# adaLN block on one Trainium2 core: the last tile's two stores move from SyncE to ScalarE, and the register that selects the general path is loaded three tiles sooner

## Chip, cores and metric

The kernel runs on one core of a Trainium2 chip. The metric is the device time of a launch in microseconds (us): the median of the runs of a kernel. The profile is one more execution, recorded instruction by instruction; its span reaches from the first recorded instruction to the last.

## What is computed

A transformer block over 2048 rows of 512 values, in bfloat16: an attention half with a softmax feature map and linear attention, and a gated feed-forward half. Both read a layer norm whose scale and shift come from the conditioning vector `c`. Cut to what matters:

```python
mod = (silu(c) @ w_mod).reshape(1, 6, 1, -1)          # sa, ca, ga, sb, cb, gb
h = layernorm(x) * (1 + ca) + sa
x = x + ga * A(h)            # q, k, v; phi = softmax(+-(q or k) @ w_phi); linear attention; @ wo
h = layernorm(x) * (1 + cb) + sb
x = x + gb * B(h)            # (sigmoid(h @ w_gate) * (h @ w_up)) @ w_down
```

The softmaxes are taken without subtracting the maximum when a bound on the logits is small enough. The kernel computes that bound on the chip (`bound_tasks`, line 896) and leaves a 0 or 1 in the one-element tile `flag` (line 915). With 0 the result stands; with 1 a general path, appended to the program behind a conditional (line 1279), recomputes everything. In the runs here the flag is 0, so the general path is jumped over.

## The kernel before

The 2048 rows are 16 tiles of 128 rows. The attention half walks over these tiles; then `downstream` runs the feed-forward half over six chunks of 1, 1, 2, 4, 4 and 4 tiles. For each chunk, TensorE makes the gate and up products for 11 slices of the 1376 hidden columns (line 850), ScalarE takes a tanh of the gate (line 854), VectorE multiplies (line 859). Then TensorE accumulates the down product of each tile over the 11 slices into a PSUM bank `y` (line 873), VectorE adds the residual and writes the bfloat16 tile `ot` (line 882, task `fin`), and SyncE stores `ot` to the output in HBM (line 884, task `st`). The last tile, t = 15, is done in two column halves of 256 (`cuts`), so it has two adds and two stores of 64 KB; all other tiles have one of each, 128 KB a store. There are two `ot` buffers.

The order of the work is planned on the host. Each step is a task with the engines that may run it and their estimated times, the keys that it reads and writes, the buffers that it holds and a due time; `Graph.order` simulates the engines and gives one list, and `emit` calls the tasks' functions in that order. An engine executes its own instructions in the order in which they were emitted; the Tile layer adds the semaphore waits. "SP" in the plan is SyncE, "ACT" ScalarE.

`load_flag` is no task of its own. It is called from inside the function of a `fin` task (line 881 stands in it) and emits a `TENSOR_LOAD` of `flag` into a register on every one of the five engines, at whatever place each engine's stream has reached (line 891). The register is read only by the compare-and-branch at line 1279. After that, each engine waits for its own work to finish and jumps over the general path to the block at the end of the program (reported as line 1306), where the engines meet. SyncE alone waits before its jump for all eight semaphores on which DMAs report, whichever engine issued them.

Of the kernel before, what the change touches and what calls it, by code (L numbers as in the profile page):

```python
# [12 lines left out]
ACT = mybir.ActivationFunctionType  # L13
# [5 lines left out]
NT = S // P  # L19
# [407 lines left out]
def kernel(  # L427
# [5 lines left out]
    pe, act, dve, pool, sp = nc.tensor, nc.scalar, nc.vector, nc.gpsimd, nc.sync  # L433
# [54 lines left out]
    o_v = out.flatten_outer_dims().rearrange("(n p) d -> p n d", p=P)  # L488
# [24 lines left out]
    def h2v(b):  # L513
        return h2_slots[b.slot].rearrange("p s k n -> p (s k) n")[:, 0:KT]

    def engine(e):
        return {"PE": pe, "ACT": act, "DVE": dve, "POOL": pool, "SP": sp}[e]
# [7 lines left out]
    def bank(name, shape=None, dtype=FP32):  # L525
        return Buf("bank", shape or [P, 512], dtype, name)
# [77 lines left out]
    def downstream(G, eT, base, first):  # L604
# [18 lines left out]
        for p, tiles in enumerate(UNITS):  # L623
# [81 lines left out]
            for q, t in enumerate(tiles):  # L705
                ub = []
                if merged:
                    us = [Buf("r2k", [P, H, DH], FP32, "u") for _ in range(2)]
                    for i in range(3):
                        for s in (i,) if i < 2 else (0, 1):  # L710
                            nh, h0, c0 = (24, 0, 0) if i < 2 else (8, 24, s)
# [127 lines left out]
        for k in range(NC):  # L839
            n = CHUNKS[k] * P  # L840
            h2k = [("h2", p, j) for p in range(len(UNITS)) if chunk_of[UNITS[p][0]] == k for j in range(KT)]
            for ft in range(FT):
                fsz = P if ft < FT - 1 else F_LAST
                g_ps, u_ps = bank("g_ps"), bank("u_ps")
                dd = gdue[k, ft]

                def f_g(e, w, ps, ft=ft, fsz=fsz, k=k, n=n):
                    h = h2v(h2[k])
                    for j in range(KT):
                        pe.matmul(ps[:fsz, 0:n], lhsT=w[:, j, ft * P:ft * P + fsz], rhs=h[:, j, 0:n], start=(j == 0), stop=(j == KT - 1))  # L850
                dur = 0.216 * n / 128
                tg = Buf("tg", [P, 512], BF16, "tg")
                G.add(f"g{k}.{ft}", {"PE": dur}, lambda e, f=f_g, ps=g_ps: f(e, wg_sb, ps), r=h2k + ["wg"], w=[("g", k, ft)], bufs=[h2[k], g_ps], due=dd)
                G.add(f"tg{k}.{ft}", {"ACT": 0.13 + n * 0.00083}, lambda e, tg=tg, g_ps=g_ps, fsz=fsz, n=n: act.activation(tg[:fsz, 0:n], g_ps[:fsz, 0:n], ACT.Tanh, scale=0.5),  # L854
                      r=[("g", k, ft)] + (["tsw"] if first else []), w=[("tg", k, ft)], bufs=[g_ps, tg], due=dd + 0.5)
                G.add(f"u{k}.{ft}", {"PE": dur}, lambda e, f=f_g, ps=u_ps: f(e, wu_sb, ps), r=h2k + ["wu"], w=[("up", k, ft)], bufs=[h2[k], u_ps], due=dd + 0.01)

                def f_hm(e, k=k, ft=ft, fsz=fsz, n=n, tg=tg, u_ps=u_ps):
                    dve.scalar_tensor_tensor(hm_all[:fsz, hm[k].slot, ft, 0:n], tg[:fsz, 0:n], 1.0, u_ps[:fsz, 0:n], op0=ALU.add, op1=ALU.mult)  # L859
                G.add(f"hm{k}.{ft}", {"DVE": 0.1 + n * 0.00115}, f_hm, r=[("tg", k, ft), ("up", k, ft)] + (["wmod_free"] if first else []),  # L860
                      w=[("hm", k, ft)], bufs=[tg, u_ps, hm[k]], due=dd + 1.0)
            nd = CHUNKS[k] * FT
            for tl in range(CHUNKS[k]):
                t = C0[k] + tl
                cuts = [(0, 256), (256, 512)] if t == NT - 1 else [(0, 512)]
                ot = Buf("ot", [P, D], BF16, "ot")
                for c0, c1 in cuts:
                    y = bank("y_ps")
                    for ft in range(FT):
                        fsz = P if ft < FT - 1 else F_LAST  # L870

                        def f_y(e, k=k, tl=tl, ft=ft, fsz=fsz, y=y, c0=c0, c1=c1):
                            pe.matmul(y[:, 0:c1 - c0], lhsT=hm_all[:fsz, hm[k].slot, ft, tl * P:(tl + 1) * P], rhs=wd_sb[:fsz, ft, c0:c1], start=(ft == 0), stop=(ft == FT - 1))  # L873
                        i = tl * FT + ft
                        due = gdue[k + 1, i * FT // nd] + 0.02 if k + 1 < NC else ydue + i * 0.216
                        G.add(f"y{t}.{ft}" + ("b" if c0 else ""), {"PE": 0.216 * (c1 - c0) / 512 + 0.0012}, f_y, r=[("hm", k, ft), ("wd", ft)],
                              w=[("y", t, c0)] + ([("ycap", t % 2)] if ft == 0 and c0 == 0 else []), bufs=[hm[k], y], due=due + c0 * 0.01)

                    def f_fin(e, t=t, y=y, ot=ot, c0=c0, c1=c1):
                        if first and t == NT - 1 and c0 == 0:  # L880
                            load_flag()
                        dve.tensor_tensor(ot[:, c0:c1], y[:, 0:c1 - c0], x1[t][:, c0:c1], op=ALU.add)  # L882
                    G.add(f"fin{t}" + ("b" if c0 else ""), {"DVE": 0.08 + 0.61 * (c1 - c0) / 512}, f_fin, r=[("y", t, c0), ("ycap", t % 2)], w=[("ot", t, c0)], bufs=[y, x1[t], ot], due=due + 1.0 + c0 * 0.01)
                    G.add(f"st{t}" + ("b" if c0 else ""), {"SP": 0.35}, lambda e, t=t, ot=ot, c0=c0, c1=c1: sp.dma_start(o_v[:, t, c0:c1], ot[:, c0:c1]),
                          r=[("ot", t, c0)], w=[("out", t, c0)], bufs=[ot], due=due + 2.0 + c0 * 0.01, nbytes=128e3 * (c1 - c0) / 512)


# [2 lines left out]
    def load_flag():  # L890
        fv_box.append(nc.values_load(flag[0:1, 0:1], min_val=0, max_val=1,
                                     skip_runtime_bounds_check_because="written as 0 or 1"))
# [26 lines left out]
    G = Graph(CAPS, DUE, REL, ENG)  # L919
# [271 lines left out]
    for cq in range(4):  # L1191
        for blk in range(4):
# [12 lines left out]
            G.add(f"qe{cq}{blk}", {"ACT": 1.0}, f_qe, r=[("q", cq, blk)], w=[("eT", cq, blk)], bufs=[qp, eT[cq]], due=due)  # L1205

    downstream(G, eT, GB, True)
    bound_tasks(G, GB + 95.0)
    order = G.order()
# [55 lines left out]
    for cq in range(4):  # L1265
        for tl in range(4):
            t = 4 * cq + tl
# [3 lines left out]
            def f_t(e, ph=ph, tp=tp):  # L1271
                for g in range(NG):
                    pe.transpose(tp[:, g, :], ph[:, g * P:(g + 1) * P], ident[:])
            G2.add(f"gT{t}", {"PE": 0.5}, f_t, r=[("gphq", t)], w=[("gT", t), "chain"], bufs=[ph, tp], due=100.0 + t)
            G2.add(f"gTc{t}", {"ACT": 1.0}, lambda e, cq=cq, tl=tl, tp=tp: act.copy(eT2[cq][:, :, tl * P:(tl + 1) * P], tp[:]),
                   r=[("gT", t)], w=[("eT", cq, tl)], bufs=[tp, eT2[cq]], due=100.0 + t)
    downstream(G2, eT2, 200.0, False)
    order2 = G2.order()
    with tc.If(fv_box[0] > 0, preferred_fallthrough_block=False):
# [31 lines left out]
```

## Time and profile before

| | us |
|---|---|
| median of 5 runs | 219.29 (218.65 to 220.47) |
| the profiled execution, its own device time | 219.26 |
| span of the profiled execution | 217.5 |
| TensorE busy in the span | 202.8 (93%) |
| VectorE busy | 165.5 (76%) |
| ScalarE busy | 112.9 (52%) |
| GpSimd busy | 98.1 (45%) |
| last matmul ends, about | 211.0 |
| last add on VectorE | 211.05 to 211.47 |

How to read it: the profiled execution is 1.7 us longer in device time than its span, and within 0.03 us of the median of the runs. Instructions are named by engine, line and operation. A "q" behind an engine's name (SPq, DVEq, PEldq) marks records of its sequencer: DMA issues, register loads, semaphore waits and branches, which are not counted as busy. The time "to landing" of a DMA runs from the start of its issue to the completion that its semaphore shows. Besides instructions, the trace holds one record for each DMA packet with its queue, size, start and duration; queue 1 carries the DMAs that SyncE issues, queue 10 those that ScalarE issues, queues 8 and 14 bring instructions.

### The profile page before, as it was taken

The numbers are of one execution on the slowest core, as the hardware profiler recorded it, in microseconds if no ns is written. First come the engines' busy times: TensorE is split into PE (matmuls) and PEld (weight loads), VectorE is DVE, ScalarE is ACT, GpSimd is POOL, SyncE is SP. The second block draws the span as 40 slices with busy tenths as digits, with TensorE's granted clock in tenths as the row PEclk, the third lists the DMA queues.
The fourth block names the chain that finished last, engine by engine and source line by source line (L and its number), as shares of the span: only waits on it lengthen the run. The fifth ranks groups of instructions, "written<-read, shape, count | busy, mean of one in ns | idle before, by whom it ended". The sixth has DMA issues, their size and how long they took to land.

```text
span 217.5 us, 4285 instructions
## 1 busy us (share of the span) xinstructions
PE 202.8 (93%) x1495; PEld 113.2 (52%) x1519; DVE 165.5 (76%) x441; ACT 112.9 (52%) x285; POOL 98.1 (45%) x125
## 2 busy tenths in 40 slices
PE   7983999999999999999999999999999999999970
PEld 2731455565565568867965444554444444444540
DVE  3898689998769999888798898999897961344230
ACT  3889499998978984424563223463112721243000
POOL 4547989999999963743542221324024100000000
PEclk9999699999999999999999999999999999999996
DMA  6999993794000111250321301133111231000111
GB/s 180 368 255 231 347 172 32 242 376 183 0 3 0 29 24 29 41 107 0 75 48 50 74 3 24 31 89 91 28 33 24 48 85 40 0 0 0 51 51 35
DMA packets 32511, 19.02 MB, mean 87 GB/s; under 512 B 21761, under 2 KB 30434, under 8 KB 32482
## 3 DMA queue, kind: packets, MB, share of 16 engines
q1 hardware_dynamic: 31952, 18.65, 32.9%
q8 instruction: 14, 0.23, 0.5%
q14 instruction: 15, 0.12, 0.2%
q10 hardware_dynamic: 530, 0.02, 0.1%
HBM read 11.58 MB, written 2.10 MB: 63 GB/s over the span
## 4 chain that ended last, share of the span: by engine, by line
PE 71%; DVE 12%; POOL 5%; ACT 3%; issue 3%; DMA 2%; SPq 0%; POOLq 0%; DVEq 0%
PE g_ps L850 18%; PE u_ps L850 18%; PE y_ps L873 17%; PE a_ps L761 6%; POOL phi L1145 5%; PE k_ps L1123 4%; PE v_ps L1127 3%; DVE st L1052 3%; DMA x_sb<-in_A_x_dram 2%; PE num L644 2%; DVE u L734 2%; DVE ks L1142 2%; PE kvacc L545 1%; DVE den L700 1%; DVE mv L1053 1%
## 5 line engine op out<-in xcount | busy, mean ns | idle before, releaser
L854 ACT ACTIVATE tg<-g_ps 128x512 bf16<-128x512 f32 (+4 forms) x66 | 29.2, 454 | 58.7 <-PE g_ps L850 33.2
L859 DVE SCALAR_TENSOR_TENSOR wmod_sb<-tg,u_ps 128x512 bf16<-128x512 bf16 (+4 forms) x66 | 32.1, 501 | 17.5 <-PE u_ps L850 9.4
L873 PE MATMUL y_ps<-wd_sb,wmod_sb 128*128 128x512 bf16 (+2 forms) x179 | 42.3, 366 | 0.3
L1145 POOL TENSOR_TENSOR phi<-e,ks 128x1024 bf16<-128x1024 bf16 (+2 forms) x22 | 31.5, 1453 | 1.5 <-ACT ks L1153 1.0
L850 PEld LDWEIGHTS <-wg_sb 128*128 128x128 bf16 (+1 forms) x264 | 23.2, 100 | 16.4
L752 POOL TENSOR_TENSOR o<-u 128x512 bf16<-128x512 f32 x14 | 17.7, 1269 | 30.2 <-DVE u L719 20.3
L850 PEld LDWEIGHTS <-wu_sb 128*128 128x128 bf16 (+1 forms) x264 | 23.1, 100 | 15.8
L873 PEld LDWEIGHTS <-wmod_sb 128*128 128x128 bf16 (+1 forms) x187 | 17.8, 98 | 15.9
L850 PE MATMUL u_ps<-wT_sb,wu_sb 128*128 128x512 bf16 (+3 forms) x131 | 25.6, 325 | 0.1
L850 PE MATMUL g_ps<-wT_sb,wg_sb 128*128 128x512 bf16 (+3 forms) x131 | 25.6, 325 | 0.1
L1142 DVE TENSOR_REDUCE ks<-e 128x64 f32<-128x1024 bf16 (+2 forms) x22 | 19.7, 909 | 2.2 <-ACT e L1139 1.3
L1139 ACT ACTIVATE e<-k_ps 128x512 bf16<-128x512 f32 (+2 forms) x44 | 18.4, 482 | 4.2 <-PE k_ps L1123 3.7
L850 PE MATMUL g_ps<-wqk_sb,wg_sb 128*128 128x128 bf16 (+5 forms) x131 | 20.1, 289 | 0.1
L850 PE MATMUL u_ps<-wqk_sb,wu_sb 128*128 128x256 bf16 (+5 forms) x131 | 19.9, 290 | 0.1
L882 DVE TENSOR_TENSOR ot<-y_ps,x 128x512 bf16<-128x512 f32 (+1 forms) x17 | 11.1, 657 | 11.4 <-PE y_ps L873 11.3
L1123 PE MATMUL k_ps<-wqk_f,h1T 128*128 128x512 bf16 x62 | 17.5, 410 | 0.8 <-DVE h1T L1105 0.8
L1202 ACT ACTIVATE eT<-q_ps 128x512 bf16<-128x512 f32 x32 | 16.9, 611 | 1.4 <-PE q_ps L1197 1.2
L1127 PE MATMUL v_ps<-wv_sb,h1T 128*128 128x512 bf16 x62 | 15.8, 380 | 1.7 <-ACT h1T L1103 1.6
L761 PE MATMUL a_ps<-wo_sb,oT 128*128 128x512 bf16 x61 | 16.3, 379 | 0.2
L1197 PE MATMUL q_ps<-h1T,wqk_f 128*128 128x512 bf16 x59 | 15.3, 379 | 0.4 <-DVE cc L701 0.2
L1052 DVE BATCH_NORM_STATS2 st<-x_sb 128x6 f32<-128x512 bf16 x16 | 10.8, 677 | 3.2 <-DMA x_sb<-in_A_x_dram 3.2
L1186 POOL TENSOR_TENSOR wd_sb<-wd_sb,wmod_sb 128x512 bf16<-128x512 bf16 x11 | 12.5, 1167 | 0.0
(148 smaller groups left out, 302.8 us busy)
## 6 DMA issues: line engine op xcount, KB each, us to landing
wmod_sb<-in_w_mod_dram SPq DMA_DIRECT2D x4, 512.0 KB, 6.0
out_dram<-ot SPq DMA_DIRECT2D x15, 128.0 KB, 1.7
x_sb<-in_A_x_dram SPq DMA_DIRECT2D x3, 512.0 KB, 9.0
wu_sb<-in_B_w_up_dram SPq DMA_DIRECT2D x1, 1376.0 KB, 6.4
wg_sb<-in_B_w_gate_dram SPq DMA_DIRECT2D x1, 1376.0 KB, 13.6
wd_sb<-in_B_w_down_dram SPq DMA_DIRECT2D x1, 1280.0 KB, 9.6
wqk_sb<-in_A_wqkv_dram SPq DMA_DIRECT2D x2, 512.0 KB, 6.7
wmod_sb<-in_w_mod_dram SPq DMA_DIRECT2D x1, 1024.0 KB, 7.5
```

Of the source, the lines that this page charges most:

```text
L752: G.add(f"o{t}", {"POOL": 1.3, "DVE": 0.62}, lambda e, ub=ub, o=o: engine(e).tensor_tensor(o[:], ub[0][:].rearrange("p h d -> p (h d)"), u ...
L761: pe.matmul(ap_[:], lhsT=oT[:, j, :], rhs=wo_sb[:, j, :], start=(j == 0), stop=(j == KT - 1))
L850: pe.matmul(ps[:fsz, 0:n], lhsT=w[:, j, ft * P:ft * P + fsz], rhs=h[:, j, 0:n], start=(j == 0), stop=(j == KT - 1))
L854: G.add(f"tg{k}.{ft}", {"ACT": 0.13 + n * 0.00083}, lambda e, tg=tg, g_ps=g_ps, fsz=fsz, n=n: act.activation(tg[:fsz, 0:n], g_ps[:fsz, 0:n ...
L859: dve.scalar_tensor_tensor(hm_all[:fsz, hm[k].slot, ft, 0:n], tg[:fsz, 0:n], 1.0, u_ps[:fsz, 0:n], op0=ALU.add, op1=ALU.mult)
L873: pe.matmul(y[:, 0:c1 - c0], lhsT=hm_all[:fsz, hm[k].slot, ft, tl * P:(tl + 1) * P], rhs=wd_sb[:fsz, ft, c0:c1], start=(ft == 0), stop=(ft ...
L1052: dve.bn_stats(st1[:, t, :], x_sb[:, t, :])
L1123: pe.matmul(kp[:], lhsT=h1T[:, j, t * P:(t + 1) * P], rhs=wqk_f[:, j, D:2 * D], start=(j == 0), stop=(j == KT - 1))
L1127: pe.matmul(vp[:], lhsT=h1T[:, j, t * P:(t + 1) * P], rhs=wv_sb[:, j, :], start=(j == 0), stop=(j == KT - 1))
L1139: act.activation(ee[:, ha:hb, s, :], kp[:, ha * DH:hb * DH].rearrange("p (h j) -> p h j", j=DH), ACT.Exp, scale=1.0 - 2.0 * s)
L1142: dve.tensor_reduce(ks[:, ha:hb].rearrange("p h s -> p (h s)"), ee[:, ha:hb].rearrange("p h s j -> p (h s) j"), axis=AX.X, op=ALU.add)
L1145: pool.tensor_tensor(ph[:, ha * 32:hb * 32].rearrange("p (h j) -> p h j", j=DH), ee[:, ha:hb].rearrange("p h s j -> p (h s) j"), ks[:, ha: ...
```

## The change

Two edits. `load_flag` is called before the add of tile 12 instead of before the first add of tile 15. And the two stores of tile 15 are planned and issued on ScalarE. Nothing else differs: compared instruction by instruction, TensorE, VectorE and SyncE have the register load at an earlier place (TensorE after the second matmul of tile 13's down product, VectorE before tile 12's add, SyncE between the stores of tiles 11 and 12), SyncE has two stores fewer, ScalarE has two stores more between its register load and its branch, and GpSimd's stream is the same. The order of the matmuls and adds is unchanged. The same two edits reach the general path, which is not executed.

```diff
                     def f_fin(e, t=t, y=y, ot=ot, c0=c0, c1=c1):
-                        if first and t == NT - 1 and c0 == 0:
+                        if first and t == NT - 4:
                             load_flag()
                         dve.tensor_tensor(ot[:, c0:c1], y[:, 0:c1 - c0], x1[t][:, c0:c1], op=ALU.add)
...
-                    G.add(f"st{t}" + ("b" if c0 else ""), {"SP": 0.35}, lambda e, t=t, ot=ot, c0=c0, c1=c1: sp.dma_start(o_v[:, t, c0:c1], ot[:, c0:c1]),
+                    G.add(f"st{t}" + ("b" if c0 else ""), {"ACT" if t == NT - 1 else "SP": 0.35}, lambda e, t=t, ot=ot, c0=c0, c1=c1: engine(e).dma_start(o_v[:, t, c0:c1], ot[:, c0:c1]),
                           r=[("ot", t, c0)], w=[("out", t, c0)], bufs=[ot], due=due + 2.0 + c0 * 0.01, nbytes=128e3 * (c1 - c0) / 512)
```

## Prediction

> **What bounds the kernel now.** I read the chain that ended last, then line by line what the sequencers do behind it. The chain first (start, duration, what):
>
> ```profile
> 199.10 1.51 PE y_ps L873 x7
> 200.61 0.05 issue
> 200.66 10.37 PE y_ps L873 x58
> 211.03 0.02 issue
> 211.05 0.42 DVE ot L882
> ```
>
> TensorE is full to 211.03, and the last add follows with no slack. No edit changes a matmul or an add, so the change can act only behind 211.47, unless it disturbs TensorE. The span ends at 217.5: 6.1 us of tail hold no computation. Lines 891 and 884 (SyncE's stores from 210 on) show what delays the stores:
>
> ```profile
> L891 PEldq TENSOR_LOAD <-flag x1: 490/490/490, 208.6 to 208.6; - x1
> L891 DVEq TENSOR_LOAD <-flag x1: 543/543/543, 210.4 to 210.4; - x1
> L891 SPq TENSOR_LOAD <-flag x1: 507/507/507, 210.9 to 210.9; - x1
> ...
> L884 SPq DMA_DIRECT2D out_dram<-ot x1: 333/333/333, 210.6 to 210.6; - x1
> ...
> L884 SPq DMA_DIRECT2D out_dram<-ot x1: 337/337/337, 211.6 to 211.6; - x1
> ...
> DMA to landing us min/median/max: 3.1/3.1/3.1
> ...
> L884 SPq DMA_DIRECT2D out_dram<-ot x1: 2044/2044/2044, 212.0 to 212.0; - x1
> ...
> DMA to landing us min/median/max: 3.2/3.2/3.2
> ```
>
> SyncE issues tile 14's store (210.563 to 210.896), then the register load holds it from 210.946 to 211.453. The first half's add had ended at 210.864, but its store is issued at 211.578; the second half's add ends at 211.478, but its store only at 212.013. That second issue takes 2.044 us where others take 0.33, and both stores land in over 3 us where tiles 12 and 13 took 1.7. Lines 1279 and 1306 tell the rest:
>
> ```profile
> L1279 PEldq COMPARE_BRANCH  x1: 3830/3830/3830, 211.2 to 211.2; - x1
> ...
> L1306 DVEq DRAIN  x1: 57/57/57, 214.4 to 214.4; - x1
> L1306 PEldq DRAIN  x1: 72/72/72, 215.1 to 215.1; - x1
> ...
> L1306 SPq EVENT_SEMAPHORE  x8: 28/28/28, 216.2 to 216.7; - x8
> ```
>
> SyncE passes the last store's completion at 215.272, five further DMA semaphores by 215.624, jumps at 215.694, is in the end block at 216.207; the engines meet and the span ends at 217.544. So landing to end costs 2.27 us, and SyncE is the last to arrive; TensorE is ready at 215.17. **The bound of the tail is the landing of the last store.**
>
> Why do stores land late? The packet records: TensorE's jump at 211.208 brings a 16 KB instruction packet on queue 8 from 212.19 to 213.68. Of the first half-store's 128 packets, 112 (14 DMA engines of 8) run at 212.42 to 212.76; 8 run by 213.3, behind an 8 KB packet of queue 14 (212.62 to 213.13, VectorE's jump); the last 8 end only at 214.14, behind the 16 KB. The second store's packets start at 214.55, after all of these: its issue had been held up until then.
>
> **What the skill says.** "DMA: Bandwidth & Descriptors", section "Issuing engines are not separate DMA queues": issuing from a second engine saves only the sequencer's time of issue, since all DMAs share 16 engines. The trace before has only two small loads from ScalarE to compare (issue 0.54 and 0.44 us, beside 0.46 and 0.45 on SyncE at that time): agrees as far as it goes. Same page, "Queues, rings and completion order": a DMA engine takes turns between queues packet by packet; the 8 packets stuck behind one 16 KB packet agree. "Runtime: NRT & Kernel Launch", "Instruction fetch mechanics": a taken branch to a target outside the loaded window must fetch it by DMA first; agrees (3.83 us for TensorE, about 2.45 for ScalarE at 200.6, 2.83 for VectorE, but 0.51 for SyncE, whose jump is short). "Perfetto Trace Analysis", "DMA Instruction — HWDGE (DVE, Sync)": the recorded issue is the sequencer's lock wait and descriptor generation, not the data; so 2.044 us is an issue that could not hand over its descriptors, as the packets show.
>
> **The change part by part.**
>
> *Register load sooner.* SyncE: 0.507 us leave the place between tiles 14 and 15; the new place is after tile 11's store (issued to 203.96) and before tile 12's at 205.476, 1.5 us of idle cover it. VectorE: 0.543 us go ahead of tile 12's add, where it waits 1.16 us for TensorE; at the old place its end (210.954) was already before the last matmul's (211.03), so nothing is won either. GpSimd and ScalarE: loaded at 172.4 and 199.9, after their last work; same place. TensorE: 0.49 us move into tile 13's matmuls. Its sequencer runs ahead: the load stood behind every matmul, yet ran at 208.58, 2.4 us before the last one ended, without a gap. The new place follows matmuls that execute about 205.0, and the last wait ahead of it is for an `hm` tile that VectorE finished at 201.23; so lead is about 3 us against 0.49. Cost nothing; uncovered it would be 0.49.
>
> *Stores on ScalarE.* ScalarE's last work ends at 200.52, so nothing is queued ahead. First half: add ends 210.864; the lag from add to issue is 0.027 (tile 14: 210.536 to 210.563), so issue at 210.89. It takes 0.34 by SyncE's rows or up to 0.54 by ScalarE's own load, so until 211.23 to 211.43. Packets start 0.84 after issue starts: 211.73, done about 212.1, just before the 16 KB packet at 212.19. Second half: add ends 211.478, issue at 211.51 (at 0.54 us for the first plus the 0.1 between two issues, 211.53). I take 211.51: 0.50 earlier than now. What does it meet? Almost exactly what the *first* half-store meets now, issued at 211.578: packets at 212.35, 0.16 after TensorE's instruction packet has begun, so one engine's 8 packets wait until 213.68. With its 3.1 us it lands at 214.65; counted from the packet's end (213.68, then 0.46 to the last packet, 0.58 to the landing) at 214.72. I take 214.70. Nothing blocks its issue: it is over by 211.85, before the instruction packet, and the first half is almost out.
>
> Sum: landing 215.27 to 214.70 is 0.57 us. The five waits, jump and meeting (2.27) stay behind it. SyncE would reach the end block at 215.64, still behind TensorE's 215.17, so the whole 0.57 counts: span 217.54 - 0.57 = 216.97, device time 219.26 - 0.57 = 218.69. The profiled run is 0.03 under the median, so **218.7 us**, -0.27%.
>
> *What moves with the stores.* Each of SyncE's two issues goes, so SyncE branches at about 211 and just waits; its queue has nothing else. ScalarE's branch moves from 200.6 to about 212.0, and its jump brings its own instruction packet (about 0.92 us later, 212.9, 0.4 long): ScalarE arrives at 214.5 with the 2.45 us of before, at 215.9 with TensorE's 3.83. The first is free; the second is 0.2 to 0.3 later than SyncE's new arrival and would halve the gain. If its packet falls on the engine that already holds TensorE's, the 8 last store packets wait some 0.4 longer: gain 0.15. These are inside the range.
>
> **The rivals.**
>
> *The store escapes the instruction packet* (packets on ScalarE's queue get their turn at once, or TensorE's fetch is elsewhere or later). Landing 1.7 after 211.51 is 213.25; SyncE is then there at 214.2 and TensorE's 215.17 becomes the bound; from the last engine's arrival to the end are 0.82 (216.728 to 217.544): span 215.99, time 217.7. Against it: in all three cases where a store's packets began 0.2 to 1.0 us after a 16 KB packet (tile 9's, landing 2.5; tile 11's, 2.4; this one, 3.1) it was held.
>
> *The wait is hidden anyway.* The second issue stalls again, as at 212.0, because the hand-over of descriptors is blocked whenever an instruction packet holds an engine, whoever issues. Then it ends about 214.06 and the store lands at 215.27 as now: 219.3. For it: ScalarE's issue overlaps tile 14's and the first half's packets. Against it: the first half-store, issued at the same moment today, took 0.337.
>
> *Slower.* SyncE's jump loses its short form. Now it takes 0.51 because the target is at hand; if SyncE's shorter stream puts the target outside what is loaded, it costs what ScalarE's (2.45) to TensorE's (3.83) does: 1.9 to 3.3 more, less 0.57, so 220.6 to 222.0. It decides only when the jump leaves the loaded instructions; SyncE's general path loses two stores too, so its distance shrinks, which speaks against it. The same end comes if TensorE's load is not covered, but for 0.49 alone that only cancels the gain.
>
> **How the numbers follow.** Forecast (218.7, by itself 218.2 to 219.2) 0.62; escape (217.7) 0.12; hidden anyway (219.3) 0.16; slower (220.6 and up) 0.10. The range leaves out the slower case alone: 217.5 to 219.7, the ends being the escape and the no-gain case with 0.2 and 0.4 for the scatter of medians (runs spread over 1.8 us). About 0.5% (1.1 us) is what a measurement of this kernel can tell from no change; the forecast is within it. Faster by more: the escape and some scatter, 0.18; within: 0.70; slower: 0.12.
>
> **What would show it.** ScalarE issues at 210.9 and 211.5, each some 0.34 long; no 2 us issue; last landing near 214.7 with 8 packets behind the 16 KB one; SyncE's jump near 215.1, still 0.5 long; TensorE's last matmul at 211.0 with no gap about its register load. Wrong if the second issue is again long, if the landing takes 1.7, if the end waits for ScalarE or TensorE, or if the last matmul moves.

## The result and the profile after

The kernel after takes 220.42 us (median; 219.77 to 221.8), the kernel before 219.37 us in the runs beside it. The ratio is 1.0055, 95% interval 1.0043 to 1.0068. The change costs 1.05 us by the medians and 1.2 by the ratio, and the time lies above the range forecast. The ratios here and below leave out runs in a slower state of the chip (two of e1, one of e14) and are no quotients of the medians shown.

Yet inside the span nearly everything went as forecast. The profiled execution of the kernel after has a span of 216.9 us, 0.64 less than before. Its device time is 219.59 us, 0.33 **more** than before. So the loss lies where the profile records no instruction: device time minus span is 1.72 us in the profiled run of before and 2.69 in that of after. Over all runs, the median of that difference is 1.73 to 1.77 before (five groups of runs) and **3.05** after, while the median spans are about the same (217.5 to 217.7 before, 217.45 after). Below, "outside" is this median of device time minus span.

The end of the chain of waits (start, duration, what):

```profile
200.40 10.37 PE y_ps L873 x58
210.77 0.02 issue
210.79 0.42 DVE ot L882
```

The 58 matmuls take 10.37 us, as before. The last add begins 0.26 earlier, a difference that arose ahead of both edits' place in the tail.

The register loads, line 891 (duration in ns as minimum/median/maximum, then first and last start in us):

```profile
L891 PEldq TENSOR_LOAD <-flag x1: 487/487/487, 201.5 to 201.5; - x1
L891 DVEq TENSOR_LOAD <-flag x1: 546/546/546, 202.7 to 202.7; - x1
L891 SPq TENSOR_LOAD <-flag x1: 511/511/511, 203.8 to 203.8; - x1
```

The loads last as long as before and start over 7 us sooner. TensorE's leaves no gap: it stands among the 58 matmuls that take 10.37 us in both kernels.

The stores of tiles 14 and 15, line 884 from 210 to 218 us:

```profile
L884 ACTq DMA_DIRECT2D out_dram<-ot x2: 351/360/369, 210.6 to 211.2; - x2
L884 SPq DMA_DIRECT2D out_dram<-ot x1: 333/333/333, 210.3 to 210.3; - x1
...
DMA to landing us min/median/max: 1.6/2.5/3.4
```

ScalarE issues the two halves 0.03 us behind their adds, in 0.37 and 0.35 us. The 2.044 us issue of before is gone. The second half still takes 3.4 us to land: TensorE's 16 KB instruction packet on queue 8 runs from 212.02 to 213.61, and the last eight store packets follow it (213.60 to 214.05).

The jumps, line 1279, and then the end block, line 1306, where the first drain of an engine is its arrival (SyncE arrives at the first of its semaphore waits):

```profile
L1279 SPq COMPARE_BRANCH  x2: 43/48/53, 210.7 to 215.1; - x2
...
L1279 ACTq COMPARE_BRANCH  x2: 38/46/53, 211.6 to 211.8; - x2
```

```profile
L1306 SPq EVENT_SEMAPHORE  x10: 17/28/28, 215.6 to 216.8; - x10
...
L1306 DVEq DRAIN  x2: 10/34/57, 214.8 to 216.4; - x2
L1306 PEldq DRAIN  x2: 8/40/73, 215.0 to 216.5; - x2
L1306 ACTq DRAIN  x2: 8/44/81, 215.0 to 216.4; - x2
```

SyncE jumps at 215.05 and is there 0.51 us later, so it keeps its short jump. ScalarE jumps at 211.80 and arrives at 215.01, 3.2 us later. Before, it arrived at 203.08, 14.5 us ahead of the span's end; now its **lead** is 1.9 us. Its line of before:

```profile
L1306 ACTq DRAIN  x2: 8/44/81, 203.1 to 217.1; - x2
```

In the meeting it still isn't the last, so inside the span this costs nothing.

One thing is new behind the span. The DMA view of the time after it, first of the kernel after, then of the kernel before:

```profile
core 0 of [0], span 216.9 us
...
DMA packets 1, 0.01 MB, mean 3 GB/s; under 512 B 0, under 2 KB 0, under 8 KB 0
...
q14 instruction: 1, 0.01, 0.8%
```

```profile
core 0 of [0], span 217.5 us
...
DMA packets 0, 0.00 MB, mean 0 GB/s; under 512 B 0, under 2 KB 0, under 8 KB 0
```

Some engine fetches 8 KB of instructions on queue 14 at 218.76 to 219.10, 1.86 us after the last recorded instruction. In the kernel before the last instruction packet ends at 217.11. Which engine this is, and what makes it late, is what the experiments had to tell.

### The profile page after: what moved, and what is told of

It is laid out like the page before. It is cut to its first block, busy times and chain, and to the rows that moved or that the text cites. A ratio compares the mean times of both kernels' runs of the same rounds, so it can differ in the third digit from the quotient of the medians.

```text
span 216.9 us, 4284 instructions
## 1 busy us (share of the span) xinstructions
PE 202.2 (93%) x1495; PEld 113.3 (52%) x1519; DVE 165.5 (76%) x441; ACT 112.9 (52%) x285; POOL 98.3 (45%) x125
## 4 chain that ended last, share of the span: by engine, by line
PE 64%; DVE 16%; POOL 7%; issue 4%; DMA 3%; ACT 2%; SPq 1%; POOLq 0%; DVEq 0%
PE g_ps L850 18%; PE u_ps L850 18%; PE y_ps L873 17%; POOL phi L1145 6%; PE a_ps L761 6%; DVE ks L1142 4%; DMA x_sb<-in_A_x_dram 3%; DVE st L1052 3%; PE num L644 2%; DVE u L734 2%; PE k_ps L1123 1%; DVE h1T L1105 1%; DVE den L700 1%; PE v_ps L1127 1%; DVE ks L1155 1%
```

## Experiments

The theories. **A**: the sooner load costs. **B**: SyncE's shorter stream (255 to 247 instructions in the program) puts its end code in a bad place. **C**: ScalarE's end code does so. Its stream grew from 699 to 705 instructions, three in the main path (two stores and a semaphore wait) and as many in the general path, and ScalarE now arrives late. **D**: DMAs on ScalarE's queue must be closed down after the end, wherever the code stands. C rests on the Trainium skill, "Runtime: NRT & Kernel Launch", section "Instruction fetch mechanics": instructions come by DMA in blocks of 16 KiB or 256 instructions, and a taken branch breaks the fetching ahead. The traces here show packets of 16 KB on queue 8 and of 8 KB on queue 14; by their times the former are TensorE's and the latter the other engines'. At the page's size of an instruction, 8 KB are 128 instructions (an estimate, which e15 puts to the test).

"Idle instructions" below are drains put into the general path, behind `emit(order2)`. They are in the program but are jumped over, so they move the code behind them and execute nothing. "Before" in a ratio is the kernel before on the same chip.

### One edit at a time

e1 is the kernel before with the sooner load alone:

```diff
-                        if first and t == NT - 1 and c0 == 0:
+                        if first and t == NT - 4:
```

> The register load three tiles sooner, both stores still on SyncE. Every theory of the lost 1.6 us that blames ScalarE (its queue, its late jump, its longer instruction stream) or SyncE's shorter stream expects none of it here: time outside the span as before, 1.7 us, and the tail's gain kept, since SyncE can issue the halves at 210.9 and 211.5 by itself: 218.7 to 218.9, ratio to before 0.997. If the sooner load itself were the cause, 220.4.

219.54 us, ratio 0.9978 (0.9957 to 0.9999), outside 1.75. Its trace on the stores:

```profile
L884 SPq DMA_DIRECT2D out_dram<-ot x3: 332/364/383, 211.2 to 212.1; - x3
...
DMA to landing us min/median/max: 3.7/3.9/4.0
```

The load isn't the cause (A falls). With the load out of the way SyncE's own issues follow their adds and take under 0.4 us; the landing was slower still, 3.7 and 4.0: the last nine packets of each half start at 214.6 only, when TensorE's 16 KB packet (213.65 to 214.61) has ended.

e2 is the kernel before with the stores alone:

```diff
-                    ... {"SP": 0.35}, lambda e, ...: sp.dma_start(o_v[:, t, c0:c1], ot[:, c0:c1]),
+                    ... {"ACT" if t == NT - 1 else "SP": 0.35}, lambda e, ...: engine(e).dma_start(o_v[:, t, c0:c1], ot[:, c0:c1]),
```

> Both stores of tile 15 on ScalarE, the register load at its old place. Theories that blame the move of the stores: time outside the span about 3.0 us, 220.4, the same as with both edits; the span about 217.0. If the loss needs the sooner load, 218.8.

220.30 us, ratio 1.0040 (1.0016 to 1.0064), outside 3.01. The stores' move brings the whole loss.

### Whose code, and where

e3 adds 8 idle instructions to SyncE in the kernel after, so that its stream has 255 again; e4 adds 122 (`act.drain()`) to ScalarE, 827 in all, exactly 128 above the 699 of before. The edit of e3:

```diff
         emit(order2)
+        for _ in range(8):
+            sp.drain()
```

> The changed kernel with 8 idle instructions added to SyncE's part of the general path, which is jumped over, so nothing more is executed and SyncE's stream is again as long as before (255 instructions, 247 in the changed kernel). Theory that the position of SyncE's code in the instruction blocks costs a fetch after the last recorded instruction: outside the span 1.7 again, time 218.8 to 219.1, and no instruction packet 2 us after the span. Theories that blame ScalarE: 220.4, unchanged.

e3: 220.21 us, ratio 1.0032 (1.0011 to 1.0053), outside 3.03. B falls.

> The changed kernel with 122 idle instructions added to ScalarE's part of the general path, jumped over: ScalarE's end code then stands at the same place within a block of 128 instructions as before (827 against 699; the changed kernel has 705). Theory that the position of ScalarE's code costs the fetch: outside the span 1.7, 218.8 to 219.1. Theories that blame SyncE's position, ScalarE's late jump or ScalarE's DMA queue: 220.4, unchanged.

e4: 219.25 us, ratio 0.9979 (0.9955 to 1.0002), outside **1.77**. Instructions that are never executed take the whole loss away. The DMA view of e4 behind its span:

```profile
core 0 of [0], span 217.9 us
...
DMA packets 0, 0.00 MB, mean 0 GB/s; under 512 B 0, under 2 KB 0, under 8 KB 0
```

The late packet is gone too, and only ScalarE's code was moved, so it was ScalarE's. D falls as it stands: e4 issues both stores on ScalarE's queue and loses nothing.

Is it a period of 128, or do any added instructions cure it? e7 adds 64 idle instructions (769), e15 adds 128 (833), e16 adds 16 (721), in the way of e4.

> The changed kernel with 64 idle instructions in ScalarE's part of the general path (jumped over; 769 instructions, half a block of 128 further on than the changed kernel's 705). Theory: the time is lost only where a block boundary lies a few instructions behind ScalarE's last recorded one, so here nothing: outside the span 1.77, time 219.2, ratio 0.998, no late instruction packet. Rival, that any late arrival of ScalarE after its DMAs costs 1.25 unless its position is just that of before: 220.4.

e7: 218.89 us, ratio 0.9983 (0.9962 to 1.0003), outside 1.72, no late packet.

> The kernel after with 128 idle instructions more in ScalarE's general path, which is jumped over: its stream is 833 instructions, one block of 128 more than the 705 of the kernel after. Block boundary theory: the end code stands at the same place in a block as in the kernel after, so the loss is back: about 3.0 us outside the span, ratio about 1.004, and a packet on queue 14 behind the span's end. Rival (a particular length or distance of the jump, or the idle instructions themselves cure it as in the kernels of 827 and 769): 1.75 us outside, ratio about 0.998, no late packet.

e15: 220.37 us, ratio 1.0056 (1.0018 to 1.0093), outside **3.05**: a whole block more, and the loss is back in full, with the late packet (2.15 us behind the span's end):

```profile
core 0 of [0], span 216.6 us
...
DMA packets 1, 0.01 MB, mean 2 GB/s; under 512 B 0, under 2 KB 0, under 8 KB 0
...
q14 instruction: 1, 0.01, 0.7%
```

> The kernel after with 16 idle instructions more in ScalarE's general path: 721 instructions. Block boundary theory: the boundary now lies ahead of the last code that ScalarE runs, so the block behind it is fetched while ScalarE still waits in the meeting, or with the jump: about 1.75 us outside the span, no packet behind its end, ratio about 0.998. If every length above 705 up to some way short of 769 pays (a long stretch of end code and not a boundary at one place): about 3.0 us outside, ratio about 1.004.

e16: 219.1 us, ratio 0.9995 (0.9978 to 1.0013), outside 1.71, no late packet. So 16 instructions are enough to leave the bad place, and e15 shows that the idle instructions as such aren't the cure. TensorE's next 16 KB packet isn't the cause either: it ends 0.19 us behind the span in the kernel after and 0.43 ahead of its end in that of before, but 0.02 ahead of it in e15 and 0.22 in e3, which lose as much.

e6 is the kernel after, with the general path's two stores left on SyncE:

```diff
-{"ACT" if t == NT - 1 else "SP": 0.35}
+{"ACT" if first and t == NT - 1 else "SP": 0.35}
```

> The changed kernel, with the general path's own last two stores left on SyncE (that path is not executed): the executed instructions are those of the changed kernel, ScalarE's stream is 701 instructions instead of 705. Theory of the position: if the place where the penalty begins lies above 701, outside the span 1.77 and time 219.2, ratio 0.998; if it lies at 700 or 701, 3.0 and 220.4. Theory that ScalarE's queue or its late jump also costs something: 219.6 or more in both cases.

ScalarE then has 701 instructions: 219.29 us, ratio 1.0002 (0.9976 to 1.0028), outside 2.27, a late packet: neither the 1.77 nor the 3.0 that I had put. Four instructions that never run are worth over half of the loss (3.05 - 2.27 = 0.78 of 1.28 us); e6 lies at the edge of the bad place.

### Is the place enough?

e5 is the kernel before with 6 idle instructions on ScalarE: 705, but ScalarE arrives 13.7 us ahead of the end.

> The kernel before with nothing of the change, only 6 idle instructions added to ScalarE's part of the general path, which is jumped over: ScalarE's stream is as long as in the changed kernel (705), every executed instruction is that of before. Theory that the position of ScalarE's end code alone costs the late fetch: 1.25 us more outside the span, 3.0 instead of 1.77, time 220.8, ratio 1.0057. Rival, that ScalarE must also arrive late at the end block (as it does with the stores), so that it has not run ahead: 219.6, ratio 1.000.

219.50 us, ratio 0.9989 (0.9967 to 1.0012), outside 1.85. The place alone costs next to nothing. Still, the packet behind the span is there, 0.98 us after its end, and so earlier than in the kernel after. The two views of e5, its last stores and the time behind its span:

```profile
L884 SPq DMA_DIRECT2D out_dram<-ot x2: 337/357/377, 211.4 to 211.8; - x2
...
DMA to landing us min/median/max: 2.7/2.8/3.0
```

```profile
core 0 of [0], span 216.8 us
...
q14 instruction: 1, 0.01, 1.0%
```

Its executed instructions are those of the kernel before, yet the second issue took 0.377 us here. So the 2.044 us on which the prediction built a part of its gain need not come in every execution. Of the traces kept, it stands in that of before alone; the last stores of all the others were issued in 0.33 to 0.41 us.

e10 is the kernel after (705) with a DMA on SyncE behind the last stores, which reads rows of `x` into the last `ot` tile (work that the computation doesn't need). It keeps the stores on ScalarE but makes the end later:

```diff
     emit(order)
+    sp.dma_start(ot_box[0][:, 0:512], x_v[:, 0, :])
```

> The changed kernel, ScalarE at the same position (705), with one load added on SyncE that waits for the last stores to land and fills their buffer again (its data is not used): the engines meet some 2 us later, ScalarE arrives when it did. Theory: ScalarE's next block, asked for about 0.6 us after it arrives, is then there before the meeting, so outside the span 1.8, while the span grows by about 2 (219.5): time 221.3. Rival, that the position or ScalarE's DMA queue costs 1.25 whenever ScalarE issued the stores: outside 3.0, time 222.5.

222.72 us, ratio 1.0181 (1.0154 to 1.0209), of which the span is 220.8; outside **1.87**. ScalarE arrives 5.5 us ahead of the end:

```profile
L1310 ACTq DRAIN  x2: 8/44/81, 215.6 to 220.6; - x2
```

The added DMA costs 3.3 us in the span where I had expected 2, so the time comes near the rival's 222.5, for another reason. But the loss outside is gone, with ScalarE's code in the same place and its stores on the same queue. What counts besides the place is how long ahead of the end ScalarE arrives.

### Is ScalarE's DMA needed?

e11 to e14 are e1 (all stores on SyncE, no DMA on ScalarE in the tail) with work on ScalarE behind the last add, so that it jumps late. e11 copies one column:

```diff
+    act.copy(ve2[:, 0:1], ot_box[0][:, 511:512])
```

> Register load sooner, stores on SyncE, and one tiny ScalarE copy (its result is not used) that waits for the last add: ScalarE arrives as late as with the stores, but issues no DMA; its stream has 700 instructions. Theory of late arrival and position: near the start of the penalty (701 gave 2.27 outside): 1.8 to 2.3 outside. If only ScalarE's DMAs cost: 1.77, time 219.3.

700 instructions, lead 3.4 us: 219.74 us, ratio 1.0013 (0.9993 to 1.0033), outside 1.81.

e12 is e11 with 5 idle instructions (705):

> As the kernel with the late ScalarE copy, with 5 idle instructions more in ScalarE's part of the general path, jumped over: 705 instructions, the position of the changed kernel, late arrival, no DMA of ScalarE. Theory of late arrival and position: outside the span 3.0, time 220.3, ratio 1.004, with an instruction packet some 2 us behind the span. If it takes ScalarE's DMA queue: outside 1.77, 219.3.

219.39 us, ratio 1.0000 (0.9974 to 1.0026), outside 1.82. This missed what my theory said (3.0). ScalarE arrived with 2.4 us of lead, 0.5 more than in the kernel after:

```profile
L1312 ACTq DRAIN  x2: 8/44/80, 215.0 to 216.8; - x2
```

Either a DMA on ScalarE was needed after all, or 2.4 us are enough. e13 tells these apart: two copies of the whole tile, and 3 idle instructions to make 705 again:

```diff
+    for _ in range(2):
+        act.copy(vaug[0][:, :, 0:DH], ot_box[0][:].rearrange("p (h d) -> p h d", d=DH))
...
         emit(order2)
+        for _ in range(3):
+            act.drain()
```

> Register load sooner, stores on SyncE, and after the last add two ScalarE copies of the whole last tile (their result is not used) instead of the tiny one: ScalarE arrives about 1 us later than with the tiny copy, some 1.4 us ahead of the end of the meeting, at the position of the changed kernel (705), and issues no DMA. Theory that it takes both lateness and position, and no DMA of ScalarE: outside the span 2.8 to 3.1, time 220.3. If ScalarE's DMAs are a needed part: 1.8 outside, 219.3.

219.99 us, ratio 1.0030 (1.0012 to 1.0048), outside **2.87**. The lead in its profile is 1.9 us, with no DMA of ScalarE in the tail:

```profile
L1313 ACTq DRAIN  x2: 8/48/87, 215.4 to 216.8; - x2
```

e14 is e13 with 67 idle instructions (769):

> The same two late ScalarE copies, with 64 idle instructions more in ScalarE's part of the general path, jumped over (769): as late, but no block boundary behind the last recorded instruction. Theory of lateness and position: outside the span 1.75, time about 219.2. If lateness alone costs: as the kernel with 705.

219.31 us, ratio 0.9991 (0.9972 to 1.0011), outside **1.73**, though ScalarE arrives later still (lead 1.2). The DMA views behind the span, e13 and then e14:

```profile
core 0 of [0], span 217.3 us
...
DMA packets 1, 0.01 MB, mean 2 GB/s; under 512 B 0, under 2 KB 0, under 8 KB 0
```

```profile
core 0 of [0], span 218.0 us
...
DMA packets 0, 0.00 MB, mean 0 GB/s; under 512 B 0, under 2 KB 0, under 8 KB 0
```

So the loss takes both a bad place of ScalarE's end code and a late ScalarE, and no DMA from ScalarE. The stream is counted in instructions of the program:

| kernel | ScalarE's stream | lead, us | packet behind the span | outside, us |
|---|---|---|---|---|
| before | 699 | 14.5 | no | 1.77 |
| e1 | 699 | 14.3 | no | 1.75 |
| e4 | 827 = 699 + 128 | 2.0 | no | 1.77 |
| e6 | 701 | 1.6 | yes | 2.27 |
| after | 705 | 1.9 | yes | 3.05 |
| e2 | 705 | 1.8 | yes | 3.01 |
| e3 | 705 | 1.6 | yes | 3.03 |
| e13 (no DMA on ScalarE) | 705 | 1.9 | yes | 2.87 |
| e15 | 833 = 705 + 128 | 1.6 | yes | 3.05 |
| e12 (no DMA on ScalarE) | 705 | 2.4 | yes | 1.82 |
| e10 | 705 | 5.5 | yes | 1.87 |
| e5 | 705 | 13.7 | yes | 1.85 |
| e11 (no DMA on ScalarE) | 700 | 3.4 | no | 1.81 |
| e16 | 721 | 1.6 | no | 1.71 |
| e7 | 769 | 1.5 | no | 1.72 |
| e14 (no DMA on ScalarE) | 769 | 1.2 | no | 1.73 |

The leads come from one execution each, so the bound between 1.9 and 2.4 us is rough.

### Without the general path

e8 is the kernel before and e9 the kernel after, each without the conditional; they leave out the recomputation for large logits, and the register load goes with it.

```diff
-    with tc.If(fv_box[0] > 0, preferred_fallthrough_block=False):
-        emit(order2)
```

> The kernel before without the general path and its branch (left out: the recomputation for large logits). No far jump, so no 16 KB instruction packet of TensorE while the last stores run. My theory of the tail: both stores issue in 0.34 us each and land in 1.7, the last at about 213.8 when the last add ends at 211.5, and the engines meet about 1 us later: 2.5 to 3 us under the kernel before, ratio 0.987. If the long landing has another cause than the instruction packet, it stays at 3.1 and only SyncE's jump (0.5) goes: ratio 0.997.

> The changed kernel without the general path and its branch (left out: the recomputation for large logits). Theory that the loss comes only from where ScalarE's end code stands behind the general path: no loss here, and a gain of some 0.5 us against the same kernel with SyncE's stores and late register load (e8): the second store is issued 0.5 sooner. If ScalarE's DMA queue itself made the launch end later: 0.7 slower than that kernel or more.

e8: 216.34 us, ratio 0.9844 (0.9807 to 0.9881), outside 1.72. e9: 216.43 us, ratio 0.9869 (0.9834 to 0.9903), outside 1.74. Against each other they show no difference. I had expected e9 to gain 0.5 us from the earlier issue, and missed: without a register load, e8's SyncE issues the last store 0.03 us behind its add already. The stores of e8, then of e9:

```profile
L884 SPq DMA_DIRECT2D out_dram<-ot x3: 332/333/409, 212.9 to 213.8; - x3
...
DMA to landing us min/median/max: 1.6/1.6/1.6
```

```profile
L884 ACTq DMA_DIRECT2D out_dram<-ot x2: 350/358/367, 211.3 to 212.0; - x2
...
DMA to landing us min/median/max: 1.6/1.6/1.6
```

With no jump every store lands in 1.6 us. From the end of the last add to the span's end it is 2.83 and 2.79 us, against 6.07 before. Of the 3.24 us between before and e8, the landing of the last store is 1.6 (3.26 to 1.62), its issue behind the add 0.5 (0.53 to 0.03), and what follows its landing 1.1 (2.27 to 1.18: semaphore waits, SyncE's jump, the meeting). So the conditional as a whole costs some 3 us of a launch although its body is skipped. That the landing's share is due to the instruction packets fits the order of the packets but isn't shown alone: e8 takes away the register load, the jump and the packets together.

## Why the prediction was wrong

What held, by its own steps. *Register load sooner*: free on every engine; TensorE's load ran 3.2 us ahead of the matmul behind it, about 3 forecast. *Stores on ScalarE*: issues 0.03 us behind the adds, 0.37 and 0.35 us long (0.34 taken), no 2 us issue, packets stuck behind TensorE's 16 KB. *SyncE's jump*: 0.51, so the slower rival with its place in SyncE was wrong, in line with e3. Of the other rivals, the escape (landing in 1.7; its 213.25 should read 213.21, which changes nothing) did not happen for the last store, nor did the second issue stall again. The profiled span came out at 216.90 for 216.97.

The **step that failed** is the sum's last: "so the whole 0.57 counts: span 217.54 - 0.57 = 216.97, device time 219.26 - 0.57 = 218.69". It carried the 1.72 us outside the span over as a constant, without a reason. It isn't one: 1.77 became 3.05 over the runs. And under *What moves with the stores* I called ScalarE's arrival at 214.5 "free", because it was ahead of SyncE in the meeting. I asked who is last in the meeting and not what each engine still has to fetch and run behind it. ScalarE's new arrival (215.01, its jump 3.2 us long instead of 2.45) was harmless in the one respect and costly in the other. No rival included that; my slower case looked at something near it, instructions that are not at hand, but at SyncE's jump ahead of the meeting and not at ScalarE behind it.

A **size was off** as well. From the last add's end to the span's end it was 6.07 us before and 5.69 after: 0.38 gained, not 0.57. The landing took 3.4 us after its issue where I took 3.2, half of it because the 16 KB packet lasted 1.59 us instead of 1.49. The other 0.26 of the profiled spans' difference lies ahead of the last add, so the agreement of the forecast span with the measured one is partly luck. Over the runs, the median spans differ by 0.05 to 0.25 us only. e5 suggests why: the long issue that I took out may be rare in the kernel before.

And no gain by the stores' move is to be seen. e1, the sooner load alone, has the ratio 0.9978 (0.9957 to 0.9999); e4 and e7, with the stores on ScalarE and no loss outside, are no better (0.9979 and 0.9983, both up to 1.000), and e16 has 0.9995. A gain of some 0.2% is at the edge of what these runs can tell. Where SyncE isn't held by its register load, it issues as promptly as ScalarE.

How far this is shown. Runs show that the loss lies outside the span, and that it takes both a late arrival of ScalarE and a bad place of its end code in blocks of 128 instructions: with leads of 1.2 to 2.0 us, 705 and 833 lose all, 701 in part, 721, 769 and 827 nothing. 699 isn't quite free of something like it: in 23 of some 200 executions of the kernel before beside the experiments, and in 7 of the 22 of e11 (700), the difference was 2.1 to 2.4 us, which the medians hide.

That ScalarE stands still behind the meeting until its next block can be used is inferred, since its instructions there aren't recorded. The packets support it in part. In every kernel with the general path a further 8 KB packet follows ScalarE's arrival by 0.6 to 0.9 us. In the kernel after it runs from 215.61 to 216.11 (a packet doesn't name its engine; the order of the arrivals does), so it has landed 0.8 us ahead of the span's end. But landing is not yet use: ScalarE's jump reached its target only 1.8 us after its packet had landed (213.22 to 215.01), in the kernel before 1.1 us (201.95 to 203.08). As an estimate from these, the next block can be used 0.3 to 1.0 us behind the span's end. In e12, whose packet landed 1.4 us ahead of the end, the same estimate gives between 0.3 ahead and 0.4 behind, and there nothing is lost. It falls short of the 1.28 us lost, so it is no full account.

The late packet itself isn't what ScalarE waits for: in e6 it ends 2.66 us behind the span, when that launch (2.36 us of device time beyond its span) is over. It fits a request for the block after the next, made when ScalarE has got through: about 1 us behind the end in e5, e10 and e12, and 1.86 to 2.3 us behind it in the kernel after, e2, e3, e6 and e15. e13's profiled execution, with the packet at 1.1 us and 2.02 us outside, was one of the lightest of its runs (2.0 to 3.3), so that trace doesn't show the usual case. Why the bound is near 2 us of lead, and where exactly the boundary lies in the end code, stays open.

## What to carry to other kernels

Read device time minus span of every version beside the span: a change that shortens the span can lose more behind it, and no view of instructions shows that. When a step moves to an engine that had been idle, its whole end moves too, jump, instruction fetch and end code, and the length of its stream shifts its end code against the block boundaries; a few idle instructions in a path that isn't executed are a cheap test of that. Of the kernels run, the sooner load with the stores left on SyncE (e1) is the simplest that avoids the loss: its ScalarE arrives 14.3 us ahead of the end, with a stream of 699. It is faster than the kernel after; whether it beats the kernel before is at the edge of the noise (0.9978, 0.9957 to 0.9999).

## What was unexpected of the hardware

- Instructions that are never executed can be worth over 1 us of a launch: 122 of them took the kernel after from 220.4 to 219.25 us, and 128 left it at 220.4. The Trainium skill, "Runtime: NRT & Kernel Launch", "Instruction fetch mechanics", calls the crossing into the next block mostly hidden. That agrees with e5 and e10 (outside 1.85 and 1.87 at 705 instructions). If the loss is such a crossing, as inferred above, it doesn't agree with a ScalarE that arrives under some 2 us before the end: there it costs 3.05 - 1.77 = 1.28 us. The page's blocks of 256 instructions aren't ScalarE's here: the loss comes back after 128 (e15) and not after 64 (e7).
- A jump over the general path, from the branch to the first instruction at its target, took ScalarE 2.45 (before) to 3.6 us (e12), TensorE 3.7 to 4.2, and SyncE 0.51 to 0.52 in every trace. Landings of 64 KB took 1.6 us in the kernels without that jump (e8, e9) and 1.6 to 4.0 in those with it.
- The long issue of 2.044 us isn't fixed by the instructions executed: e5 executes the same ones and issued in 0.377 us (one trace of each).
